# A pre-LN attention and SwiGLU block on one core: projection sums in row halves, and more of the score maxima moved ahead of attention

## The chip, the core and the metric

The kernel runs on one core of a Trainium2 chip. The metric is the device time of one execution in microseconds, the median over runs; lower is better.

## The reference

The input is one sequence of 2048 tokens of width 640. All arithmetic is float32.

```python
h  = x + mha(layernorm(x), wqkv, wo)        # 32 heads of width 20, softmax(q k^T / sqrt(20)) v
h2 = h + (silu(z @ w_gate) * (z @ w_up)) @ w_down      # z = layernorm(h), hidden width 1728
```

The softmax needs, for every query and head, the largest score over 2048 keys, to be subtracted before the exponential.

## The kernel before

Precision is kept by splitting each float32 operand into a high part in the matmul format `F32R` and a low part, so that each projection is a sum of three terms over five slices of 128 rows: 15 products of 128 rows.

There are three stages. In the **projections** (code in the block from line 252 to 556) the 2048 tokens are taken in four chunks of 512, `c` = 0 to 3. For each chunk a list `work` gives an order of 18 steps: ten blocks of 128 columns of queries or keys (`query_key`, line 416, matmul on line 424) and eight half value tiles (`value`, line 453, matmul on line 461). Each finished block is evicted by `keep`, split into high and low part, and stored to DRAM from the ScalarE queue; from there `stack` (line 136) loads it head by head into tiles of keys and queries, in which two heads share a matmul tile: one on rows 0 to 59 or 61, the other on rows 64 to 123 or 125. The next chunk's layer norm and its transposes (`flip`, line 389) are done between the steps.

In **attention** (from line 970) a unit `u` is one group of four heads with one chunk of 512 queries: 8 groups x 4 chunks = 32 units, of 16 key tiles each. Per key tile there are four score products of 128 keys by 512 queries (`scores`, line 890, matmul on line 895), four exponentials on ScalarE (line 901), and the weighting of the values (`weigh`, line 905), which runs two tiles later. The maximum is subtracted inside the score product: two extra rows of the query tile hold the negated maximum in high and low part, against rows of ones in the key tile, so all of a unit's maxima must be known before its first score.

The maxima need their own products, of 128 queries by 512 keys, reduced by VectorE. Counted per unit, key chunk `kc` of 512, query tile `t` and head pair `pair`, there are 1024 pairs (a pair is two heads, two products). `in_projections` (line 220) names those that are done during the projections by `max_pair` (line 166): two products into one tile of two PSUM banks, one reduction over 128x1024. There are 208 of them, on tiles of keys and queries staged early in the four `raw` buffers. `visit` (line 344) puts up to three of them after each step. The other 816 pairs, 1632 single products, are done by `max_one` (line 177) during attention, ahead of the unit that needs them.

The order in attention is written out by hand for each key tile by a string:

```python
ORDER = ("SmsSMMsWMm", "SsSmWmMs", "SssMWmS")
```

`s` and `S` are scores on the lower and the upper row half, `m` and `M` maxima on the lower and upper half, and `W` is the weighting together with the other work (weights for the next stage are prepared there too). Tile number modulo 3 chooses the string. When the maxima are used up the order is `sSsSW`. PSUM in this stage has four banks for scores, three for maxima, one for the weighting.

After attention come the output projection, the second layer norm and the feed-forward part, which the change does not touch. The order of the instructions on each engine is that of the program (`tc.manual_schedule()`).

Of the kernel before, what the change touches and what calls it, by code (L numbers as in the profile page):

```python
# [17 lines left out]
P = 128  # L18
# [3 lines left out]
DH = 20  # L22
# [17 lines left out]
ORDER = ("SmsSMMsWMm", "SsSmWmMs", "SssMWmS")  # L40
# [3 lines left out]
def tile_block(ctx: ExitStack, tc: tile.TileContext, x, wqkv, wo, wg, wu, wd, out):  # L44
# [21 lines left out]
    psum = ps_ctx.enter_context(tc.tile_pool(name="psum", bufs=1, space=bass.MemoryType.PSUM))  # L66

    def ps_wide():
        return psum.tile([P, 2, CH], F32, name="ps_wide", tag="ps_wide", bufs=3)

    def ps_one():
        return psum.tile([P, CH], F32, name="ps_one", tag="ps_one", bufs=2)
# [56 lines left out]
    def fill_ones(k):  # L129

        for b in range(2):
            nc.gpsimd.memset(k[b * ROW + ROW // 2 : (b + 1) * ROW].bitcast(F32), 1.0)
# [30 lines left out]

    mxs = {u: stk.tile([P, 2, 2, TPC, NC], F32, name=f"mx{u}") for u in range(NU)}

    def max_pair(mx, q, k, pair, t, kc, k0):

        ps = ps_wide()
        for b in range(2):
            rows = slice(b * ROW, b * ROW + NPART)  # L170
            nc.tensor.matmul(  # L171
                ps[:, b, :], q[rows, pair, t * P : (t + 1) * P], k[rows, pair, k0 : k0 + CH],
                start=True, stop=True,
            )
        nc.vector.tensor_reduce(mx[:, :, pair, t, kc], ps, axis=AX.X, op=ALU.max)  # L175
# [71 lines left out]

    def next_e():
        es.append(es.pop(0))
        return es[-1]  # L250

    with tc.tile_pool(name="pa", bufs=2) as pa:
# [18 lines left out]
        slot = [0]  # L271
        items, place, users = [], {}, {}

        def stored_at(which, g, c):

            block = ((g + 1) * GD - 1) // P
            if c == 0:
                return 2 * block + 4
            if c < NC - 1:
                return 18 * c + 3 + 3 * block + (0 if which else 1)  # L280
            return 18 * c + 3 + block + (0 if which else ND)
# [4 lines left out]
        def stage(use, which, g, c):  # L286
            place[which, g, use] = len(items)
            users[len(items)] = 0
            items.append([which, g, c, None, None])

        def load_items():
            for n, (which, g, c, loaded, _) in enumerate(items):
                if loaded is not None:
                    continue
                if slot[0] < stored_at(which, g, c) or (n >= 4 and users[n - 4]):
                    return
                t = raw_tile().rearrange("p a b -> p (a b)")[:, : 2 * CH].rearrange(
                    "p (h n) -> p h n", h=2
                )
                stack(t, which, g, slice(c * CH, (c + 1) * CH))  # L300
                items[n][3:] = t, slot[0]

        def staged_keys(g, c, kc):
            k, q = place[1, g, (c, kc)], place[0, g, c]

            def one(t, pair):
                max_pair(mxs[g * NC + c], items[q][3], items[k][3], pair, t, kc, 0)
                for n in (k, q):
                    users[n] -= 1
                load_items()  # L310

            def ready():
                return all(items[n][3] is not None and slot[0] >= items[n][4] + 2 for n in (k, q))

            pairs = [(t, pair) for t in moved(g * NC + c, kc) for pair in range(2)]
            for n in (k, q):
                users[n] += len(pairs)
            return [(ready, lambda a=a: one(*a)) for a in pairs]

        def unit_keys(u, kc, t, pair):  # L320
            max_pair(mxs[u], queries[u], keys[0], pair, t, kc, kc * CH)
            if u == 0 and (kc, t, pair) == (NC - 1, TPC - 1, 1):
                max_all(0)

        def in_unit(u, kc, at):
            return [
                (lambda: at <= slot[0], lambda t=t, pair=pair: unit_keys(u, kc, t, pair))
                for t in moved(u, kc) for pair in range(2)
            ]

        for g in range(1, NG):
            stage((0, 0), 1, g, 0)
            stage(0, 0, g, 0)
        for g in range(1, NG):
            stage((1, 0), 1, g, 0)
            stage(1, 0, g, 1)
            stage((1, 1), 1, g, 1)
        urgent = [a for kc in range(NC) for a in in_unit(0, kc, 18 * kc + 7)]
        early = [a for g in range(1, NG) for a in staged_keys(g, 0, 0)]
        early += in_unit(1, 0, 28) + in_unit(1, 1, 28)  # L340
        early += [a for g in range(1, NG) for kc in range(2) for a in staged_keys(g, 1, kc)]
        early += in_unit(2, 0, 46) + in_unit(2, 1, 46)

        def visit(n):
            load_items()
            for _ in range(n):
                for queue in (urgent, early):
                    if queue and queue[0][0]():
                        queue.pop(0)[1]()
                        break  # L350
# [13 lines left out]
        def split_w(m):  # L364
            cs = slice(m * P, (m + 1) * P)
            engine = nc.gpsimd if m % 2 == 1 else nc.vector
            split(raws.pop(m), w_hi[:, :, cs], w_lo[:, :, cs], engine)

        def norm(c):
# [4 lines left out]
            def apply(t):  # L374
# [9 lines left out]
                [lambda t=t: stats(pa, xs[c * TPC + t], mv[:, t, :]) for t in range(TPC)]  # L384
                + [lambda f=f, g=g: (f(), g()) for f, g in zip(steps[::2], steps[1::2])]
                + [lambda t=t: apply(t) for t in range(TPC)]
            )

        def flip(c, k):
            ps = ps_one()  # L390
# [4 lines left out]
            z_hi, z_lo = (z[:, k, :] for z in zs[c])  # L395
            split_sbuf(ps, z_hi, z_lo, next_e()[:, 0].bitcast(F32))
# [13 lines left out]
        def store(*last, queue=nc.scalar):  # L410

            while stores:
                queue.dma_start(*stores.pop(0))
            stores.extend(last)

        def query_key(c, *ms):

            z_hi, z_lo = zs[c]
            pss = [ps_one() for _ in ms]
            n = 0  # L420
            for a, w in ((z_hi, w_hi), (z_lo, w_hi), (z_hi, w_lo)):
                for ps, m in zip(pss, ms):
                    for k in range(ND):
# [4 lines left out]
                        if n == 1 and k == 3 and c:  # L428
                            visit(1)
                n += 1  # L430
            for ps, m in zip(pss, ms):
                keep(c, m, ps)

        def keep(c, m, ps):

            e = next_e()
            if slot[0] < 8:
                split(ps, e[:, 0], e[:, 1], nc.vector)
            else:
                split_sbuf(ps, e[:, 0], e[:, 1], e[:, 1].bitcast(F32))  # L440
            r0 = m // 2 * P
            pieces, r = [], r0
            while r < r0 + P:
# [3 lines left out]
                pieces.append(  # L447
# [1155 lines left out]
```

## Time and profile before

| | us |
|---|---|
| median of 3 runs | 2115.23 |
| lowest and highest run | 2113.74, 2119.4 |
| span of the profiled execution | 2118.2 |
| first score product of attention starts at | 343.1 |
| last copy of a weighted sum starts at | 1550.6 |

The page gives the profiled execution by its span alone; it lies 3.0 us above the median. In the rows below, PE is TensorE's matmuls, PEld its weight loads, DVE is VectorE, ACT ScalarE, POOL GpSimd, SP SyncE. A row of the timeline gives start, duration, engine, line, operation, tiles written and read, sizes, the count of merged instructions, and in brackets the idle time before it with what ended it. A row of the groups gives count, busy time and mean duration in ns, then idle time before. A row of the stretches gives, for each engine, busy time and number of instructions.

### The profile page before, as it was taken

How to read it: one execution, taken by the hardware profiler on the slowest of the kernel's cores; microseconds unless marked ns; L12 is line 12 of the kernel's file. 1: busy time of each engine (PE TensorE's matmuls, PEld its weight loads, DVE VectorE, ACT ScalarE, POOL GpSimd, SP SyncE). 2: the span in 40 equal slices, each digit the busy share in tenths (PEclk: the TensorE clock that was granted, in tenths of full speed). 3: DMA queues.
4: the chain of work that ended last, by engine and by line, in shares of the span. 5: the costliest groups of instructions: out<-in, count | busy, mean ns of one | idle time of the engine just before them, and what ended most of it. 6: DMA issues, size and time to landing. Idle time of an engine off the chain costs nothing.

```text
span 2118.2 us, 35577 instructions
## 1 busy us (share of the span) xinstructions
PE 2079.0 (98%) x12606; PEld 1205.0 (57%) x12606; DVE 1752.2 (83%) x2901; ACT 1295.4 (61%) x2571; POOL 705.0 (33%) x1009
## 2 busy tenths in 40 slices
PE   7998999999999999999999999999999999999998
PEld 5766675333333333333333333335578888888888
DVE  6998897999999999999999999996358766666677
ACT  3222215999999999999999999996743222212221
POOL 3221212244334433353420001001135534663555
PEclk9999999999999999999999999999999999999999
DMA  7555533333442534534332113132137755884542
GB/s 248 176 172 154 164 123 90 118 104 126 126 139 82 175 99 125 164 134 141 129 116 67 41 34 90 34 94 81 35 118 255 269 164 191 296 306 157 191 155 93
DMA packets 199673, 295.27 MB, mean 139 GB/s; under 512 B 46840, under 2 KB 81656, under 8 KB 198472
## 3 DMA queue, kind: packets, MB, share of 16 engines
q1 hardware_dynamic: 185912, 266.77, 38.9%
q10 hardware_dynamic: 13584, 26.23, 4.1%
q8 instruction: 101, 1.65, 0.3%
q14 instruction: 76, 0.62, 0.1%
HBM read 196.44 MB, written 95.68 MB: 138 GB/s over the span
## 4 chain that ended last, share of the span: by engine, by line
PE 87%; DVE 7%; DMA 4%; issue 1%; SPq 1%; ACT 1%; POOL 0%; ACTq 0%; POOLq 0%; DVEq 0%
PE acc L905 24%; PE ps_max L181 15%; PE ps_one L895 15%; PE ps_a L1068 14%; PE ps_b L1162 7%; PE ps_one L424 4%; DVE mx L175 4%; PE ps_max L633 2%; PE ps_wide L171 2%; PE ps_one L461 2%; DMA halves<-j_d 1%; PE ps_b L633 1%; DMA qk_d<-e 1%; DVE mx L187 1%; DMA units<-w_d 0%
## 5 line engine op out<-in xcount | busy, mean ns | idle before, releaser
L901 ACT ACTIVATE probs<-ps_one 128x512 f32<-128x512 f32 x2048 | 1045.2, 621 | 132.8 <-PE ps_one L895 128.1
L187 DVE TENSOR_REDUCE mx<-ps_max 128x1 f32<-128x512 f32 x1632 | 1020.5, 682 | 95.3 <-PE ps_max L181 52.8
L895 PE MATMUL ps_one<-q_stk,k_stk 62*128 62x512 f32 x2048 | 551.0, 421 | 0.7 <-ACT e L265 0.7
L905 PE MATMUL acc<-probs,v_stk 128*32 128x512 f32 x4096 | 546.1, 605 | 0.3
L181 PE MATMUL ps_max<-k_stk,q_stk 60*128 60x512 f32 x1632 | 541.3, 460 | 2.4 <-DVE mx L187 1.5
L181 PEld LDWEIGHTS ps_max<-k_stk,q_stk 60*128 60x128 f32 x1632 | 230.5, 184 | 429.3 <-DVE mx L187 413.1
L895 PEld LDWEIGHTS ps_one<-q_stk,k_stk 62*128 62x128 f32 x2048 | 300.0, 185 | 80.5 <-ACT probs L901 51.6
L175 DVE TENSOR_REDUCE mx<-ps_wide 128x2 f32<-128x1024 f32 x208 | 240.7, 1217 | 20.1 <-PE ps_wide L171 19.7
L1283 DVE TENSOR_TENSOR tmp<-ps_a,tmp 128x512 f32<-128x512 f32 x208 | 141.2, 689 | 120.3 <-PE ps_a L1068 94.5
L1162 PE MATMUL ps_b<-halves,yp 128*128 128x320 f32 x1032 | 179.3, 308 | 2.0 <-DMA halves<-j_d 1.3
L1162 PEld LDWEIGHTS ps_b<-halves,yp 128*128 128x128 f32 x1032 | 165.1, 188 | 18.6 <-POOL yp L81 1.5
L905 PEld LDWEIGHTS acc<-probs,v_stk 128*32 128x32 f32 x4096 | 80.7, 108 | 160.0 <-issue 152.0
L1068 PE MATMUL ps_a<-t,units 128*128 128x512 f32 x624 | 162.7, 396 | 0.0
L198 POOL CAST both<-neg 128x16 fp32r<-128x16 f32 x32 | 6.6, 208 | 466.8 <-DVE neg L194 222.8
L1068 PE MATMUL ps_a<-z,units 128*128 128x512 f32 x516 | 133.8, 394 | 0.0
L1068 PEld LDWEIGHTS ps_a<-t,units 128*128 128x128 f32 x624 | 112.6, 188 | 18.8 <-ACT tmp L1296 0.2
L81 POOL TENSOR_TENSOR yp<-y,yp 128x256 fp32r<-128x256 f32 x96 | 60.4, 629 | 188.2 <-ACT yp L80 188.2
L1167 DVE TENSOR_TENSOR h<-ps_b,h 128x320 f32<-128x320 f32 x248 | 110.0, 480 | 6.9 <-PE ps_b L1162 5.4
L1068 PEld LDWEIGHTS ps_a<-z,units 128*128 128x128 f32 x516 | 93.1, 187 | 15.9
L1068 PE MATMUL ps_a<-z,lasts 128*128 128x512 f32 x324 | 92.5, 393 | 0.0
L80 ACT ACTIVATE yp<-tmp 128x512 fp32r<-128x512 f32 x40 | 25.3, 632 | 103.2 <-POOL tmp L1155 103.2
L265 ACT ACTIVATE e<-ps_one 128x512 f32<-128x512 f32 x31 | 18.5, 598 | 105.4 <-PE ps_one L424 81.0
(164 smaller groups left out, 2066.1 us busy)
## 6 DMA issues: line engine op xcount, KB each, us to landing
units<-w_d SPq DMA_DIRECT2D x186, 256.0 KB
w_d<-stage SPq DMA_DIRECT2D x106, 256.0 KB
halves<-j_d SPq DMA_DIRECT2D x70, 320.0 KB
j_d<-stage SPq DMA_DIRECT2D x42, 320.0 KB
raw<-qk_d SPq DMA_DIRECT2D x70, 160.0 KB
k_stk<-qk_d SPq DMA_DIRECT2D x64, 160.0 KB
q_stk<-qk_d SPq DMA_DIRECT2D x64, 160.0 KB
rb<-r_d SPq DMA_DIRECT2D x32, 256.0 KB
```

The source lines that it names most:

```text
L175: nc.vector.tensor_reduce(mx[:, :, pair, t, kc], ps, axis=AX.X, op=ALU.max)
L181: nc.tensor.matmul(ps, queries[u][rows, pair, t * P : (t + 1) * P], keys[u // NC][rows, pair, kc * CH : (kc + 1) * CH], start=True, stop=True,
L187: nc.vector.tensor_reduce(mxs[u][:, b, pair, t, kc : kc + 1], ps, axis=AX.X, op=ALU.max)
L424: nc.tensor.matmul(ps, w[:, k, m * P : (m + 1) * P], a[:, k, :], start=(n == 0 and k == 0), stop=(n == 2 and k == ND - 1),)
L633: nc.tensor.matmul(ps[:, :HALF], a[:, k, :], w[:, k, hs], start=(n == 0), stop=(n == 3 * ND - 1),)
L895: nc.tensor.matmul(ps, keys[u // NC][rows, p, kt * P : (kt + 1) * P], queries[u][rows, p, :], start=True, stop=True,)
L901: nc.scalar.activation(probs[p][:, b, :], ps, AF.Exp, scale=scale)
L905: nc.tensor.matmul(acc[32 * j : 32 * j + 32, :], values[u // NC][:, kt, j * VW : j * VW + 32], probs[j // 2][:, j % 2, :], start=(kt == 0) ...
L1068: nc.tensor.matmul(ps.rearrange("p (t n) -> p t n", t=TPC), w[k][:, i], z[k][:, :, j], start=(first and m == 0), stop=(last and m == len(n ...
L1162: nc.tensor.matmul(ps, a, b, start=(n == 0), stop=(n == len(pairs) - 1))
L1167: nc.vector.tensor_tensor(out=h, in0=ps, in1=h, op=ALU.add)
L1283: add = lambda out, ps, x: nc.vector.tensor_tensor(out=out, in0=ps, in1=x, op=ALU.add)
```

## The change

**Projections, sums.** Each product of 128 rows becomes two products of 64 rows, rows 0 to 63 and 64 to 127 of the same operands. A sum is a job: first its 15 lower halves, then its 15 upper halves, into the same PSUM bank. The first upper half waits for an empty instruction on ScalarE, which waits for the last lower half. A class `Halves` writes out the order: it keeps a planned time for each row half and engine, issues the upper halves of one job between the lower halves of the next, and puts products for maxima in wherever its plan has banks free. The first two blocks stay whole.

**Projections, maxima.** For two keys a and b, max(q·a, q·b) = q·a + max(0, q·(b - a)). GpSimd subtracts one half of the staged keys from the other: within a chunk (72 pairs: ScalarE takes the positive part of 256 columns, VectorE adds the other 256 and takes the maximum in one pass), or one chunk from another (224 pairs' worth: one product with the differences, 512 columns through ScalarE, a second product with the plain keys, added and maximised by VectorE). 296 pairs' worth are done here instead of 208, on more places for staged keys: four quarters of the still unused key tile among them.

**Projections, queues.** PSUM is cut into five single banks and three for sums. The stores of blocks and values go out from the SP queue instead of ScalarE's.

**Attention.** 728 pairs are left, 1456 single products. Each key tile has three maxima, in six orders whose row halves alternate from one product to the next. The rest of attention is as before.

```diff
-ORDER = ("SmsSMMsWMm", "SsSmWmMs", "SssMWmS")
+ORDER = ("sMsSmSmW", "SmMsMsSW", "mSmMsSsW")
+ORDER += tuple(a.swapcase().replace("w", "W") for a in ORDER)
...
+    def max_differences(mx, q, k, pair, t, kc, place):
+
+        pss = max_products(q, k, pair, t, 0)
+        more = place.rearrange("p (i n) -> p i n", i=2)
+        for b, ps in enumerate(pss):
+            nc.scalar.activation(more[:, b], ps[:, CH // 2 :], AF.Relu)
+        for b, ps in enumerate(pss):
+            nc.vector.tensor_tensor_reduce(
+                out=more[:, b], in0=ps[:, : CH // 2], in1=more[:, b], scale=1.0, scalar=LEAST,
+                op0=ALU.add, op1=ALU.max, accum_out=mx[:, b, pair, t, kc : kc + 1],
+            )
+
+    def max_twice(mx, q, first, more, pair, t, kc, b, place):
...
+        def second():
+            product(pss[1], first)
+            nc.vector.tensor_tensor_reduce(
+                out=place, in0=pss[1], in1=place, scale=1.0, scalar=LEAST,
+                op0=ALU.add, op1=ALU.max, accum_out=mx[:, b, pair, t, kc : kc + 1],
+            )
+
+        product(pss[0], more)
+        nc.scalar.activation(place, pss[0], AF.Relu)
+        return second
...
-        if u == 0 or (u == 2 and kc < 2) or (c < 2 and kc == 0):
+        if u == 0 or (c == 1 or u == 2) and kc < 2:
             return True
-        return c == 1 and kc == 1 and t < (2 if g < NG // 2 else 3)
+        return c == 0 and kc <= (2 if g % 2 else 0)
...
+            def issue(self, half):
+                job = next(j for j in self.jobs if j["at"][half] < j["n"])
+                i = job["at"][half]
...
+                rows = slice(half * ROW, (half + 1) * ROW)
+                lhs, rhs, out = job["step"](i, rows)
+                product = nc.tensor.matmul(
+                    job["ps"][:, :out], lhs, rhs,
+                    start=(half == 0 and i == 0), stop=(half == 1 and i == job["n"] - 1),
                 )
...
+                self.stream(half, out / 2217)
+                if half == 0 and job["at"][0] == job["n"]:
+                    job["after"] = nc.scalar.nop().ins
+                    behind(job["after"], product.ins)
...
+                if half == 1 and job["at"][1] == 1:
+                    behind(product.ins, job["after"])
...
+            def run(self, c, n, step, done):
+                job = dict(c=c, n=n, step=step, done=done, at=[0, 0], ps=None)
+                self.jobs.append(job)
...
+                while job["at"][0] < n:
+                    half = int((self.second[1] or self.may_follow()) and self.t[1] <= self.t[0])
+                    if self.second[half]:
+                        self.finish_second(half)
+                    else:
+                        self.issue(half)
+                    self.pair()
...
-        def store(*last, queue=nc.scalar):
-
+        def store(*last, queue=nc.sync):
...
-        def query_key(c, *ms):
+        def query_key(c, m):
 
             z_hi, z_lo = zs[c]
...
+            def step(i, rows):
+                a, w = terms[i // ND]
+                return w[rows, i % ND, cs], a[rows, i % ND, :], CH
+
+            pe.run(c, 3 * ND, step, lambda ps: keep(c, m, ps))
...
-            order = ORDER[now[0] % 3] if singles[0] or singles[1] else "sSsSW"
+            order = ORDER[now[0] % len(ORDER)] if singles[0] or singles[1] else "sSsSW"
```

More of the change, by code (lines that the diff above doesn't have):

```diff
@@ L334, in tile_block @@
[L334 to L350, printed above, removed]
+        own_places = [None, quarters[0]]
@@ L352, in tile_block, with behind @@
+        def behind(ins, other):
+            tc.add_manual_dep(
+                ins, other.name,
+                mybir.DependencyInfo(mybir.DependencyClass.Sync, mybir.DependencyReason.DATA),
+                reason="the second half after the first",
+            )
+        pe = Halves()
+        landed = {(i, g, c): 0 for i in range(2) for g in range(NG) for c in range(NC)}
         raws = {}
@@ L476, in tile_block @@
+            pe.run(c, 3 * ND, step, done)
         load_x(0)
         fill_ones(k_stk[0])
+        for u in range(NU):
+            if any(moved(u, kc) for kc in (1, 2)):
+                nc.gpsimd.memset(mxs[u], LEAST)
         for i in range(4):
```

457 lines of the change are left out of this document (349 added, 108 removed).

## The prediction

> **What bounds the kernel now.** I read the busy time by stretch first, then the timeline of each stage. The change touches the projections (start to 343 us) and attention (343 to 1551 us); what follows is untouched.
>
> ```profile
> core 0: us, PE busy (x) PEld busy (x) DVE busy (x) ACT busy (x) POOL busy (x), PEclk, DMA share, GB/s
> 0.00:50.00 50.00, 38.32 (x152) 28.10 (x152) 32.21 (x71) 18.11 (x27) 19.07 (x16) 0.97 0.80 253
> 50.00:343.10 293.10, 279.30 (x1433) 197.59 (x1431) 259.55 (x281) 71.95 (x129) 60.00 (x48) 0.99 0.51 155
> 100.00:150.00 50.00, 47.24 (x229) 31.20 (x230) 48.92 (x67) 10.36 (x18) 9.03 (x7) 1.00 0.61 182
> 300.00:320.00 20.00, 19.87 (x123) 15.41 (x123) 19.90 (x19) 3.00 (x8) 0.42 (x2) 1.00 0.15 59
> 379.00:451.00 72.00, 71.98 (x490) 28.05 (x489) 66.24 (x110) 65.29 (x131) 26.86 (x50) 1.00 0.41 124
> L187 DVE TENSOR_REDUCE mx<-ps_max 128x1 f32<-128x512 f32 x1632 | 1020.5, 682 | 95.3 <-PE ps_max L181 52.8 <-PE ps_one L895 27.9 <-ACT e L80 10.5
> ```
>
> In the projections' rows from 100 and from 300 us DVE is 98 and 99% busy while ACT does 21 and 15%: the maxima set the pace there. In attention PE never stops, DVE is at 92% and ACT at 91%. Three engines at that level hold each other up, so I go to the single key tile. W (line 905, the weighting) closes each tile.
>
> ```profile
> 700.42 1.06 PE L905 MATMUL acc<-probs,v_stk 128*32 128x512 f32 x8
> 701.42 0.19 PEld L181 LDWEIGHTS ps_max<-k_stk,q_stk 60*128 60x128 f32 x2 [0.84 <-DVE mx L187]
> 701.42 0.50 PE L181 MATMUL ps_max<-k_stk,q_stk 60*128 60x512 f32 x2
> 701.95 3.78 DVE L187 TENSOR_REDUCE mx<-ps_max 128x1 f32<-128x512 f32 x6 [0.22 <-PE ps_max L181]
> 702.32 1.06 PE L905 MATMUL acc<-probs,v_stk 128*32 128x512 f32 x8
> 703.32 0.51 PE L181 MATMUL ps_max<-k_stk,q_stk 60*128 60x512 f32 x2
> 704.08 4.52 ACT L901 ACTIVATE probs<-ps_one 128x512 f32<-128x512 f32 x9 [0.33 <-PE ps_one L895]
> 704.45 1.06 PE L905 MATMUL acc<-probs,v_stk 128*32 128x512 f32 x8
> 705.44 0.49 PE L181 MATMUL ps_max<-k_stk,q_stk 60*128 60x512 f32 x1
> 707.14 1.07 PE L905 MATMUL acc<-probs,v_stk 128*32 128x512 f32 x8
> 154.59 0.97 PE L171 MATMUL ps_wide<-k_stk,q_stk 60*128 60x512 f32 x6
> 384.73 0.63 ACT L915 ACTIVATE o<-acc 128x512 f32<-128x512 f32 x1
> 858.50 0.68 ACT L915 ACTIVATE o<-acc 128x512 f32<-128x512 f32 x1
> ```
>
> Three tiles run from W at 700.42 to W at 707.14: 6.72 us, 2.24 a tile. W itself holds PE 1.00 us (702.32 to 703.32). Between the W's stand the products over 60 to 62 rows: 6 in 0.90 us (701.42 to 702.32), 7 in 1.13, 9 in 1.70 (705.44 to 707.14). A lower-half and an upper-half product run side by side: the two loads at 701.42 take 0.19 us together and the two products 0.50. Three pairs take 0.97 (154.59), so one more pair costs (0.97 - 0.50)/2 = 0.235 us, which I call a slot. By the orders on line 40 the gap of 6 is M m S s S m, three slots, 0.70; that of 7 is m M S s S s M, four slots, 0.94; both leave about 0.2 for switching to W. The gap of 9 (m S S m s S M M s) has five slots and should take 1.37; it takes 0.33 more. That is the stall: five maxima in one tile for three PSUM banks, at (3.78 - 0.68)/5 = 0.62 us of DVE each (0.68 being one reduction, line 187). Between units there is more: 13 units of 16 tiles from 384.73 to 858.50 are 36.44 us each, of which 16 x 2.24 = 35.84 are tiles and 0.60 the unit's own work.
>
> **Attention after.** Each of the six new orders has four scores and three maxima, halves strictly alternating. Seven products are four slots, so the gap should be the 1.13 us of today's gap of 7, and the tile 2.13. DVE needs 3 x 0.62 = 1.86 us of it; ACT needs four exponentials at (4.52 - 0.62)/8 = 0.49, 1.95 us. Both fit, and the maxima come one by one, so the 0.33 us stall goes. What is late next is PE itself, with ACT 0.18 us behind. A unit becomes 16 x 2.13 + 0.60 = 34.7 us, 1.76 less; over the 30 units before the output projection mixes in, 53 us. The ends: nothing, if the three engines go on stalling each other, and ACT's 1.95 us, if W's switch hides (another 16 x 0.18 x 30 = 86 us). I take the 2.13 because that gap of 7 is measured with the same products. Maxima finish no later: 1456 at 3 a tile last 485 tiles, as 1632 at 10 in 3 lasted 490, and the tightest unit keeps 5 tiles in hand in both. Attention's DMAs and the weight preparation hang on tiles, not on time; they move closer together at a DMA share of 0.41.
>
> **Projections after: PE.** The changed kernel's PE queue holds two whole blocks, 38 block sums and 32 value sums as 30 half products each, 296 pairs of max products (72 by differences inside a chunk, 224 by differences between two chunks) and 60 transposes.
>
> ```profile
> 13.22 1.59 PEld L402 LDWEIGHTS ps_wide<-ident,xt 128*128 128x128 f32 x14 [0.56 <-issue]
> 17.18 2.56 PE L424 MATMUL ps_one<-z_hi,w_hi 128*128 128x512 f32 x10 [0.79 <-ACT z_hi L80]
> 28.08 1.30 PE L424 MATMUL ps_one<-z_hi,w_hi 128*128 128x512 f32 x5
> 29.22 1.30 PE L424 MATMUL ps_one<-z_lo,w_hi 128*128 128x512 f32 x5
> 149.91 0.66 PE L392 MATMUL ps_one<-ident,xt 128*128 128x128 f32 x4
> 150.32 1.40 PE L424 MATMUL ps_one<-z_hi,w_hi 128*128 128x512 f32 x5
> 294.82 0.89 PE L461 MATMUL ps_one<-w_lo,z_hi 128*128 128x320 f32 x5
> 295.55 0.90 PE L461 MATMUL ps_one<-w_hi,z_lo 128*128 128x320 f32 x5
> 343.10 0.49 PE L895 MATMUL ps_one<-q_stk,k_stk 62*128 62x512 f32 x1 [0.69 <-ACT e L265]
> ```
>
> Five block products follow in 1.14 us (28.08 to 29.22), 0.228 each; five value products in 0.73, 0.146 each; a flip takes 0.41 (149.91 to 150.32). Before: 17.2 us to the first block, 40 x 15 x 0.228 = 137, 32 x 15 x 0.146 = 70, 208 x 0.235 = 49, 15 x 0.41 = 6: 279 of the 343.1 us; 64 are waits. After, if halves pair like the maxima: 88 more pairs, 21 us, so 300 with no waits at all. Two half products of the same length cost one whole one, so the halves by themselves gain nothing; they let a single half max product fill in.
>
> **Projections after: DVE, ACT, POOL, SP.**
>
> ```profile
> L175 DVE TENSOR_REDUCE mx<-ps_wide 128x2 f32<-128x1024 f32 x208 | 240.7, 1217 | 20.1 <-PE ps_wide L171 19.7
> L1283 DVE TENSOR_TENSOR tmp<-ps_a,tmp 128x512 f32<-128x512 f32 x208 | 141.2, 689 | 120.3 <-PE ps_a L1068 94.5 <-POOL yp L81 14.7 <-ACT tmp L1296 4.5
> L1185 DVE TENSOR_TENSOR own<-ps_b,own 128x320 f32<-128x320 f32 x128 | 56.7, 481 | 2.5 <-PE ps_b L1162 2.4
> L80 ACT ACTIVATE yp<-y 128x256 fp32r<-128x256 f32 x96 | 30.6, 362 | 78.8 <-DVE y L1287 66.8 <-DMA units<-w_d 8.4 <-PE ps_b L1162 3.5
> L81 POOL TENSOR_TENSOR e<-e 128x512 fp32r<-128x512 f32 x22 | 28.4, 1291 | 122.2 <-ACT e L80 86.2 <-DMA raw<-qk_d 31.1 <-PE ps_wide L171 4.8
> 0.82 0.06 DVE L77 MEMSET eps_t<- 128x1 f32 x1 [0.82 <-PEq L1586]
> 9.02 0.17 DVE L90 TENSOR_SCALAR v_a<-mv 128x4 f32<-128x4 f32 x1
> 9.23 0.17 DVE L90 TENSOR_SCALAR r_a<-v_a 128x4 int32<-128x4 int32 x1
> 145.77 7.53 SPq L143 DMA_DIRECT2D raw<-qk_d  x8
> 146.03 1.35 ACTq L413 DMA_DIRECT2D qk_d<-e  x3
> ```
>
> DVE's 208 reductions go (240.7 us). In come 224 add-and-max passes over 512 columns and 144 over 256, each followed by a write of its 128x1 result. No pass of that kind is in this trace. From below: the reduction's 0.62 us, 0.34 for half the columns (0.62 less 256 x 1.08 ns, the slope between the tensor-tensor rows of 512 and 320 columns), result hidden: 139 + 49 = 188 us. From above: 0.69 and 0.41 plus a small operation's step of 0.21 (9.02 to 9.23): 202 + 89 = 291 us. I take 0.06 (the smallest write) on top of the mean of the two prices, 0.72 and 0.44, 225 us, since 128x1 is nearest to the memset: less DVE than today, for 296 pairs instead of 208. [...]
>
> ACT gets 224 relus of 512 at 0.49 and 144 of 256 at about 0.30 (0.362 less overlap), 153 us, in a stage where it was idle for four fifths; it loses the issue of 107 stores (0.45 each, row at 146.03), 48 us. POOL gets 37 subtractions, 48 us at 1.29, and 14 small memsets while it is idle at the start. SP gets the 112 stores and 248 instead of 168 loads; at 7.53/8 = 0.94 us, waits included, that is at most 340 us, and at 0.45 net 160 us. Behind a store that waits for POOL's low part stand the loads of the next keys; the products wait for those. I cost it at nothing while the net figure holds; the cover is the time between a load and its first use.
>
> The added waits: a sum's second half waits for an empty instruction on ACT, which itself waits for the end of the first half. Behind it on PE stands everything; on ACT, relus and evictions. It is hidden while the next sum's first half has products to issue. The swap of the PSUM pool at the start costs under 1 us, the wait for the last eviction of the first flips.
>
> From 50 us on DVE has 259.6 - 240.7 = 19 us of other work and ACT 72, so the sums there are 244 for DVE and 225 for ACT. PE needs 300 over the whole stage. No engine is full any more, but the queues are in order. I let half of today's 64 us of waits stay: 300 + 32 = 332, 11 us less than 343, which leaves DVE at 244 of 282 us. The ends are 300 (43 less) and 364 (21 more).
>
> **The sum.** The profiled execution has a span of 2118.2 us, 3.0 above the 2115.23 median of the runs. 2118.2 - 53 - 11 = 2054; on the median's scale 2051.
>
> **Rivals.**
> - DVE stays the bound of the projections: at the upper price 291 + 19 = 310 us after the first 50, at the 97% of its busiest stretches 320. The rows at 98 and 99% speak for it, the memset's 0.06 against it. Stage 370 us, 38 more than I forecast: 2089. Chance 0.15.
> - Weight loads bound the halves. Where loads set the pace, one follows the other in (1.59 - 0.19)/13 = 0.108 us (13.22). If the two halves' loads queued, a value sum would take 30 x 0.108 = 3.24 us for 2.19, 34 us over 32 sums: 2085. The two loads in 0.19 us at 701.42 speak against it. [...] Chance 0.05.
> - Attention falls to ACT's pace, 2.05 a tile or less: another 40 to 86 us, near 2000. Today's tiles of 1.90 speak for it; they live on the slower tile before them. Chance 0.07.
> - Slower: the handover between halves. 70 sums each wait for ACT, which now has about 2.2 us of relus per sum in front. If PE finds no other half product, each sum loses that: it eats the 64 us gained from 0.9 us per sum on, and at 2 us adds 140: 2190. For it speaks that PE's queue is in order, against it that the next sum's fifteen first halves fill 3.4 us. Chance 0.12.
> - The change does not do what it says: attention keeps 2.24 a tile and the projections their 343: 2115. Chance 0.03.
>
> **The numbers.** My forecast has the remaining 0.58: 2051, by itself 2025 to 2075. The range 2010 to 2098 takes in the DVE and load rivals and leaves out 0.22 or slightly less. Measurement can tell about 0.3% (6 us) from no change. Faster: 0.58 + 0.15 + 0.05 + 0.07 = 0.85; same 0.03; slower 0.12.
>
> **What would show it.** In the profile after: W to W 2.13 us in all tiles with maxima, units of 34.7 us, PE's waits for attention's reductions gone; first score near 332 us; the new passes near 0.72 and 0.44 us apart and DVE below 90% in the projections; load pairs of the halves together in 0.19 us. The forecast is wrong if W to W stays above 2.2, if the first score comes after 364 us, or if PE's waits at the second halves reach 0.9 us per sum.

## The result, and the profile after

After: 2080.53 us, median of 4 runs (2077.16 to 2086.12). Before, on the same chip: 2115.86 (2113.74 to 2119.4). The ratio is 0.9833, 95% interval 0.981 to 0.9856: about 35 us faster, where 64 were forecast. The profiled execution spans 2084.3 us against 2118.2, 33.9 less. The changed kernel's is the slowest of its four (2086.12), 5.6 us above the median, so figures of its trace lie some us high. Three kernels of experiments 5 and 6 have the same projections as the changed one; their first scores come at 365.7, 367.7 and 368.5, so a first score is good to about 4 us.

Busy time of the changed kernel by stretch (columns as named in the first row):

```profile
core 0: us, PE busy (x) PEld busy (x) DVE busy (x) ACT busy (x) POOL busy (x), PEclk, DMA share, GB/s
50.00:369.70 319.70, 298.59 (x2593) 264.12 (x2593) 228.06 (x811) 237.78 (x499) 126.85 (x105) 0.94 0.59 181
159.00:176.10 17.10, 16.10 (x137) 13.94 (x135) 8.74 (x26) 13.09 (x24) 6.46 (x5) 1.00 0.49 148
176.10:186.30 10.20, 5.82 (x40) 5.83 (x41) 2.71 (x8) 4.24 (x8) 3.78 (x3) 0.50 0.40 109
369.70:1522.00 1152.30, 1148.04 (x7915) 466.02 (x7916) 961.11 (x1610) 1084.80 (x2141) 326.34 (x533) 1.00 0.33 104
```

The two stages went opposite ways. Attention's first score comes at 369.70 instead of 343.1: the projections are 26.6 us longer, where 11 less were forecast. From there to the last copy of a weighted sum (1520.7, before 1550.6) attention takes 1151.0 us instead of 1207.5, 56.5 less, about as forecast. What follows is 4.0 shorter. In the projections PE's granted clock is 0.94 in place of 0.99, and for 10.2 us it is 0.50.

Attention, the timeline of PE over three key tiles (W is line 1235, scores 1225, maxima 223):

```profile
700.10 1.07 PE L1235 MATMUL acc<-probs,v_stk 128*32 128x512 f32 x8
702.22 1.06 PE L1235 MATMUL acc<-probs,v_stk 128*32 128x512 f32 x8
703.21 0.49 PE L1225 MATMUL ps_one<-q_stk,k_stk 62*128 62x512 f32 x1
703.22 0.73 PE L223 MATMUL ps_max<-k_stk,q_stk 60*128 60x512 f32 x2
704.34 1.06 PE L1235 MATMUL acc<-probs,v_stk 128*32 128x512 f32 x8
706.45 1.06 PE L1235 MATMUL acc<-probs,v_stk 128*32 128x512 f32 x8
771.97 0.50 PE L1225 MATMUL ps_one<-q_stk,k_stk 62*128 62x512 f32 x1
775.71 0.47 PE L223 MATMUL ps_max<-k_stk,q_stk 60*128 60x512 f32 x1 [2.70 <-DMA q_stk<-qk_d]
```

From 700.10 to 706.45 three tiles take 6.35 us, 2.12 each, and PE has no wait in them; 2.12 is the median in each of the six orders. The first 28 units are 34.1 to 35.5 us but for one of 39.18, that of the last row: there a maximum waited 2.70 us for queries that had not landed, and 3.4 us of half clock followed.

The new passes on DVE, 512 columns (line 210) and 256 (line 193):

```profile
211.93 0.69 DVE L210 CUSTOM_DVE_ANT_0 q_stk<-ps_single,q_stk 128x512 f32<-128x512 f32 x1
212.54 0.08 DVE L210 DVE_READ_ACCUMULATOR2_ANT mx<- 128x1 f32 x1
212.54 0.69 DVE L210 CUSTOM_DVE_ANT_0 v_stk<-ps_single,v_stk 128x512 f32<-128x512 f32 x1
62.16 0.42 DVE L193 CUSTOM_DVE_ANT_0 v_stk<-ps_single,v_stk 128x256 f32<-128x256 f32 x1
62.51 0.08 DVE L193 DVE_READ_ACCUMULATOR2_ANT mx<- 128x1 f32 x1
62.51 0.42 DVE L193 CUSTOM_DVE_ANT_0 v_stk<-ps_single,v_stk 128x256 f32<-128x256 f32 x1
```

One follows the other in 0.61 and 0.35 us. The read of the accumulator (0.08) starts with the next pass and adds nothing to that: the plain reductions of 512 columns before followed each other in 0.62.

What PE's weight loads waited for in the projections (total us, times, longest), first before, then after:

```profile
PEld ps_wide L171 <- DVE mx L175: 29.4, 60, 2.2
PEld ps_wide L171 <- issue: 13.3, 51, 0.5
PEld ps_one L424 <- issue: 11.0, 44, 0.4
```

```profile
PEld ps_single L180 <- DVE mx L193: 7.5, 6, 3.2
PEld ps_one L498 <- ACT v_stk L311: 5.8, 2, 5.6
PEld ps_single L204 <- ACT e L311: 4.9, 2, 4.3
PEld ps_single L204 <- DVE mx L210: 4.3, 16, 0.9
PEld ps_one L498 <- issue: 2.7, 13, 0.4
```

Before, the waits were many and short: 60 for reductions, and some hundred "issue" waits at changes between products of 128 and of 60 rows. Both are mostly gone. In their place stand a few long ones, of which several end on ACT's evictions. Two weight loads of different row halves run side by side, as the prediction expected, 0.19 us for both:

```profile
287.17 0.19 PEld L498 LDWEIGHTS ps_one<-z_lo,w_hi 64*128 64x128 f32 x1
287.17 0.19 PEld L498 LDWEIGHTS ps_one<-z_hi,w_lo 64*128 64x128 f32 x1
```

The longest wait, in the rows of ACT, SP and POOL around it:

```profile
165.28 3.16 SPq L151 DMA_DIRECT2D k_stk<-qk_d  x4
166.69 0.60 ACT L311 ACTIVATE v_stk<-ps_one 128x512 f32<-128x512 f32 x1 [0.28 <-issue]
168.03 1.29 POOL L89 TENSOR_TENSOR v_stk<-v_stk 128x512 fp32r<-128x512 f32 x1 [1.23 <-ACT v_stk L88]
168.49 4.25 SPq L151 DMA_DIRECT2D raw<-qk_d  x8
173.07 1.70 SPq L691 DMA_DIRECT2D qk_d<-v_stk  x2
173.23 0.63 ACT L88 ACTIVATE z_hi<-e 128x512 fp32r<-128x512 f32 x1
179.83 0.60 ACT L311 ACTIVATE v_stk<-ps_one 128x512 f32<-128x512 f32 x1 [5.97 <-DMA qk_d<-v_stk]
```

A block is evicted at 166.69 into the third of three rotating buffers (it lies in the tile `v_stk`), its low part is ready at 169.3, its store issued only at 173.07, and the next eviction that draws this buffer waits for the landing until 179.83. PE stops from 174.79 to 180.48, and its clock is halved from 176.1 to 186.3 (the row above).

The stage also has a new end. Behind the last product of the sums, at 359.40, the order still holds 21 max products, and the first score comes 10.3 us later; before the change none was left there, and it came 1.1 us later. The clock is halved again from 363.84, although no step from one product's start to the next in the 6.9 us before is longer than 0.95 us:

```profile
363.10 5.61 PE L204 MATMUL ps_single<-raw 60*128 60x512 f32 x14 [0.20 <-ACT q_stk L216]
363.84:369.70 5.86, 4.87 (x13) 2.81 (x13) 5.18 (x16) 4.18 (x7) 0.00 (x0) 0.50 0.25 71
```

This half clock lasts until 377.5, 7.8 us into attention.

For the accounts below I split PE's time from the first block product (at 17.2 us before, 17.9 after) to the first score into steps over 0.6 us from one product's start to the next ("pauses"), the time at half clock outside them, and the rest, at full clock. A straight-line fit of the steps to the kinds of product gives the pace per product in us; it moves by 0.01 to 0.03 with the length of the stretches that are fitted.

| | first score | pauses (count) | half clock | rest | pace: block, value, max |
|---|---|---|---|---|---|
| before (whole sums) | 343.1 | 21.9 (17) | 6.8 | 297.2 | 0.243, 0.149, 0.20 |
| after (halves) | 369.7 | 31.1 (17) | 31.2 | 289.5 | 0.133, 0.076, 0.105 |

Before, 416 max products at 0.20 are 83 us of PE; after, 592 at 0.105 are 62. Pairing works. What the stage loses is pauses and half clock: 9 and 24 us more.

### The profile page after: what moved, and what is told of

Its sections match the earlier page's. It is cut to its first block, busy times and chain, and to the rows that moved or that the text cites. A ratio compares the mean times of both kernels' runs of the same rounds, so it can differ in the third digit from the quotient of the medians.

```text
span 2084.3 us, 39077 instructions
## 1 busy us (share of the span) xinstructions
PE 2037.9 (98%) x13656; PEld 1245.0 (60%) x13656; DVE 1617.8 (78%) x3251; ACT 1471.6 (71%) x2941; POOL 774.7 (37%) x1082
## 4 chain that ended last, share of the span: by engine, by line
PE 89%; DMA 7%; DVE 1%; issue 1%; POOL 1%; SPq 1%; ACT 1%; POOLq 0%; ACTq 0%; DVEq 0%
PE acc L1235 24%; PE ps_one L1225 16%; PE ps_a L1398 15%; PE ps_max L223 11%; PE ps_b L1492 8%; PE ps_one L498 7%; PE ps_single L204 3%; PE ps_max L963 2%; DMA k_stk<-qk_d 1%; PE ps_b L963 1%; DMA raw<-qk_d 1%; DMA halves<-j_d 1%; DMA q_stk<-qk_d 1%; DMA qk_d<-e 1%; PE ps_single L180 1%
## 5 line engine op out<-in xcount | busy, mean ns | idle before, releaser
L1231 ACT ACTIVATE probs<-ps_one 128x512 f32<-128x512 f32 x2048 | 1057.6, 611 | 66.5 <-PE ps_one L1225 26.3
L229 DVE TENSOR_REDUCE mx<-ps_max 128x1 f32<-128x512 f32 x1456 | 915.7, 684 | 124.9 <-PE ps_max L223 76.4
L1225 PE MATMUL ps_one<-q_stk,k_stk 62*128 62x512 f32 x2048 | 586.5, 432 | 1.0 <-DVE mx L210 1.0
L223 PE MATMUL ps_max<-k_stk,q_stk 60*128 60x512 f32 x1456 | 486.1, 440 | 3.4 <-DMA q_stk<-qk_d 3.4
L1225 PEld LDWEIGHTS ps_one<-q_stk,k_stk 62*128 62x128 f32 x2048 | 289.8, 186 | 291.3 <-ACT probs L1231 269.6
L223 PEld LDWEIGHTS ps_max<-k_stk,q_stk 60*128 60x128 f32 x1456 | 241.4, 185 | 169.2 <-DVE mx L229 131.6
L210 DVE CUSTOM_DVE_ANT_0 q_stk<-ps_single,q_stk 128x512 f32<-128x512 f32 x158 | 105.7, 689 | 50.9 <-ACT q_stk L216 40.1
L498 PE MATMUL ps_one<-z_hi,w_lo 64*128 64x512 f32 x380 | 104.5, 401 | 0.0
L216 ACT ACTIVATE q_stk<-ps_single 128x512 f32<-128x512 f32 x158 | 91.6, 596 | 17.8 <-PE ps_single L204 9.4
L1270 POOL TENSOR_TENSOR o<-o,rb 128x512 f32<-128x512 f32 x31 | 39.9, 1286 | 164.7 <-DMA q_stk<-qk_d 84.3
```

What stands on the lines that cost most here:

```text
L210: nc.vector.tensor_tensor_reduce(out=place, in0=pss[1], in1=place, scale=1.0, scalar=LEAST, op0=ALU.add, op1=ALU.max, accum_out=mx[:, b, p ...
L216: nc.scalar.activation(place, pss[0], AF.Relu)
L223: nc.tensor.matmul(ps, queries[u][rows, pair, t * P : (t + 1) * P], keys[u // NC][rows, pair, kc * CH : (kc + 1) * CH], start=True, stop=True,
L229: nc.vector.tensor_reduce(mxs[u][:, b, pair, t, kc : kc + 1], ps, axis=AX.X, op=ALU.max)
L498: product = nc.tensor.matmul(job["ps"][:, :out], lhs, rhs, start=(half == 0 and i == 0), stop=(half == 1 and i == job["n"] - 1),)
L1225: nc.tensor.matmul(ps, keys[u // NC][rows, p, kt * P : (kt + 1) * P], queries[u][rows, p, :], start=True, stop=True,)
```

## The experiments

**1. The stores' queue.** Theory Q blamed the move of the stores to SP.

```diff
-        def store(*last, queue=nc.sync):
+        def store(*last, queue=nc.scalar):     # second kernel: nc.gpsimd
```

> The changed kernel with one word altered: the projections' stores are issued from ACT's queue again, as before the change, instead of SP's. Theory Q (queue): on SP a store stands behind loads that themselves wait, an eviction buffer comes free late, ACT's next eviction waits for it (5.97 us at 175 us into the changed kernel), PE runs dry and its clock is halved afterwards; so the first score comes at 335 to 350 us instead of 369.7, and the whole takes 2045 to 2065 us. Theory M (the plan's assumed times are too short wherever the stores are issued) and theory W (the stage is simply that much work): first score within 5 us of 369.7, time within 6 us of 2080.

> The changed kernel with the projections' stores on GpSimd's queue. Theory Q: no loads are ahead of the stores here, only the low parts and the subtractions of keys, so the first score comes at 340 to 360 us and the whole takes 2050 to 2070 us. Theories M and W: first score within 5 us of 369.7, time within 6 us of 2080. If an issue on this queue is dear for GpSimd itself (it also makes the low parts that PE needs), the stage is longer than 370 us.

Third, the kernel before with its stores on SP:

> The kernel before with the projections' stores issued from SP's queue, nothing else altered. Theory Q: its first score moves from 343 to 353 to 373 us, with new waits of ACT's evictions for stores. Theory M: within 5 us of 343, since its own plan leaves the buffers time enough. A result in between (5 to 10 us) says that the queue alone costs something and the rest comes from the fuller plan.

ACT's queue: 2105.08 us (0.9942, 0.9918 to 0.9965), first score 386.9. GpSimd's: 2116.87 (0.9995, 0.9979 to 1.0012), first score 396.3. Before with SP stores: first score 341.6, 2118.96 in one run. Q falls: away from SP the changed kernel is 25 and 36 us slower, and SP costs the old one nothing that one run shows. Theories M and W, by which the queue makes no difference, missed for the changed kernel as well: its first score comes 17 and 27 us later. With ACT's queue, waits of ACT (totals), and the same buffer again:

```profile
ACT q_stk L216 <- POOL z_lo L89: 8.9, 2, 6.4
ACT v_stk L311 <- DMA qk_d<-v_stk: 5.7, 1, 5.7
172.77 0.79 ACTq L691 DMA_DIRECT2D qk_d<-v_stk  x2
179.01 0.60 ACT L311 ACTIVATE v_stk<-ps_one 128x512 f32<-128x512 f32 x1 [5.67 <-DMA qk_d<-v_stk]
```

ACT's relus (line 216) now wait for low parts that POOL makes; no relu reads those, a store in front of it in ACT's queue does. And the wait for this buffer's store to land is there whichever queue issues it: 5.97 us from SP, 5.67 from ACT's, 9.47 from GpSimd's (there the eviction starts at 189.37). So the queue alone does not make it late.

**2. Issue sooner.** Two ways to shorten the time from low part to store: on SP as soon as the plan takes the data to be ready, and on GpSimd right behind the low part.

```diff
             def issue(self, half):
+                if stores and self.now() >= due[0]:
+                    store()
...
             store(*pieces)
+            due[0] = max(free, pe.free["pool"]) + 0.3
...
```

```diff
-            store(*pieces)
-            kept[id(e)] = 1
+            store()
+            for dst, src, what in pieces:
+                nc.gpsimd.dma_start(dst, src)
+                landed[what[0]] += what[1]
```

> The changed kernel with each of the projections' stores issued on SP as soon as the plan takes its data to be ready, instead of with the next sum's end or when its buffer comes round again. In the changed kernel and in the one with ACT's stores alike, the pause at 175 us follows a store issued 1 us before its buffer is wanted, so ACT waits out the whole landing (5.97 and 5.67 us). Theory D (late issue): the pauses at 72, 148, 175 and 305 us (1.8, 4.2, 5.7 and 2.8 us) go, with the half clock behind them (about 12 us lost), so the first score comes at 345 to 356 us and the whole takes 2055 to 2068. Theory S (the store meets a busy SP queue or busy DMAs whenever it is issued): first score within 5 us of 369.7, time within 6 us of 2080.

> The changed kernel with each block's stores issued on GpSimd right behind the low part that GpSimd has just made, so that they wait neither for SP's loads nor for the next sum's end; values' stores stay on SP. Theory D (what hurts is the time from the low part to the issue): the pauses at 72, 148, 175 and 305 us shrink by 2 to 4 us each, first score 352 to 362, the whole 2062 to 2074. If GpSimd's issue takes its time from the low parts and the differences of keys (80 issues at about 0.6 us, 48 us), pauses that end on GpSimd's operations appear instead and the first score is over 370.

The first: 2090.02 (0.9868, 0.9846 to 0.989), first score 375.6; the second 2091.04 (0.9883, 0.9862 to 0.9905), 376.5. Theory D falls in both, and theory S, which had the time unchanged within 6 us, missed as well. On SP the store still leaves at 172.62 behind twelve loads and the pauses at 149, 175 are as before; the one at 201 us grows from 1.6 to 4.9, ending on differences of keys whose eight loads take SP 6.87 us to issue instead of 5.05. On GpSimd five of the pauses over 1.3 us end on its own operations (one in the changed kernel), as the second branch of the expectation had it. There the store of the buffer at 175 us leaves right behind its low part, and still the eviction waits 5.0 us for the landing, 9.3 us after the first issue:

```profile
171.66 1.19 POOL L747 DMA_DIRECT2D qk_d<-v_stk  x2 [0.29 <-POOL v_stk L89]
180.97 0.60 ACT L311 ACTIVATE v_stk<-ps_one 128x512 f32<-128x512 f32 x1 [5.00 <-DMA qk_d<-v_stk]
```

An early issue does not make this buffer free in time.

**3. The ring.** Leave the time of issue alone; take the transposed blocks out of the buffers.

```diff
-                self.single.append([self.use("scalar", 0.5, self.now() + 0.4) + 0.2])
-                self.use("scalar", 0.48)
-                self.use("pool", 1.3, self.free["scalar"] + 0.1)
+                seen = self.use("scalar", 0.5, self.now() + 0.4)
+                self.single.append([self.use("vector", 0.68, seen + 0.1) + 0.2])
...
-            split_sbuf(ps, z_hi, z_lo, next_e()[:, 0].bitcast(F32))
+            split(ps, z_hi, z_lo, nc.vector)
```

The first lines are the plan's booking of a transposed block: it changes with the edit, and with it the order of products that the plan writes out.

> The changed kernel, with the transposed blocks of x split straight from PSUM (high part by ACT, low part by DVE) instead of through a copy in one of the three eviction buffers. Theory R (the ring): in chunks 1 to 3 two transposes and one block go through three buffers, so a block's buffer comes round again one block later, before its store has landed; taken out of the ring, the pauses at 148 and 175 us (4.2 and 5.7 us) and the half clock behind them (17 us long, 8 lost) go, those at 72 and 305 us, where blocks follow blocks, stay. First score 350 to 358, the whole 2060 to 2070. DVE gets 15 x 0.69 = 10 us more, POOL 19 less. Theory S (stores wait for SP and busy DMAs, whatever the ring): first score within 5 us of 369.7, time within 6 us of 2080.

2063.38 us (0.9751, 0.9736 to 0.9765), first score 349.39. Theory R held, with a first score just below its range. Waits of ACT for stores between 50 and 350 us, the changed kernel's first, then this kernel's, with PE's longest wait and the stage:

```profile
ACT e L311 <- DMA qk_d<-e: 8.1, 2, 5.7
ACT v_stk L311 <- DMA qk_d<-v_stk: 6.0, 1, 6.0
ACT z_hi L311 <- DMA qk_d<-z_hi: 3.2, 1, 3.2
```

```profile
ACT e L311 <- DMA qk_d<-e: 1.9, 1, 1.9
ACT v_stk L311 <- DMA qk_d<-v_stk: 0.9, 1, 0.9
ACT ev L761 <- DMA v_d<-ev: 4.6, 2, 3.3
PEld ps_one L1224 <- DVE mx L210: 3.2, 1, 3.2
50.00:349.39 299.39, 286.28 (x2592) 256.51 (x2593) 237.91 (x826) 229.06 (x485) 107.98 (x90) 0.98 0.62 192
```

The waits for stores out of the ring, 17.3 us, became 2.8; new are 4.6 us for the stores of values, which have buffers of their own (`ev`). In the changed kernel the four waits of the first list ended PE's pauses at 72, 148, 175 and 305 us, 14.5 us together. Of these the second and third are gone, the first is 1.3 us, and the one at 305, expected to stay, lost its wait for a store (3.0 us are left there, behind a relu). All pauses fall from 31.1 to 19.9 us (11), half clock from 31.2 to 10.2, the clock rises to 0.98; PE's products still take 301 us at full clock. Of the 20.3 us that the first score gained, 11.2 are pauses and 10.5 the half clock's loss (half of 31.2 less 10.2); the rest of the stage gives back 0.8, and it starts 0.6 later. By the medians of the runs the gain is 17.2.

Not all of it is the ring's. 13.6 us are gained up to the last product of the sums, where the pauses for stores were. The other 6.7 lie behind it: the new order leaves 3 max products there instead of 21, and then PE waits 3.2 us for DVE's last maxima (last row but one). The edit also takes 15 splits off ACT and POOL. A fourth buffer with the old order would separate these; it was not run.

**4. Halves or whole sums.** The halves are taken back, and with them the empty instruction; all else stays.

```diff
-                rows = slice(half * ROW, (half + 1) * ROW)
-                lhs, rhs, out = job["step"](i, rows)
+                lhs, rhs, out = job["step"](i, slice(0, P))
...
```

> The changed kernel with its block and value sums as whole products of 128 rows again, with no handover between halves; maxima, plan and attention unchanged. Theory P (pairing): outside pauses a max product takes 0.105 us on PE after the change and 0.20 before it, because a lone half product only finds a partner among half products; without halves 592 of them cost 56 us more and the sums some 12 us less, so the first score comes at 400 to 420 us and the whole takes 2110 to 2135. Theory H (the handover eats the halves' gain): the first score comes before 365 us.

2383.59 us in one run, first score 662.0. P has the sign, and its price was far too low. Stretches of this kernel:

```profile
50.00:190.00 140.00, 138.32 (x584) 83.50 (x582) 81.13 (x341) 82.90 (x204) 48.65 (x39) 0.97 0.54 167
191.50:345.00 153.50, 153.50 (x305) 74.79 (x304) 52.29 (x158) 51.62 (x90) 20.30 (x17) 0.50 0.24 74
358.70:638.00 279.30, 279.30 (x565) 137.24 (x565) 89.03 (x279) 95.98 (x173) 43.23 (x39) 0.50 0.18 55
```

At full clock the max products stand mostly in twos between products of 128 rows (71 of the 93 groups up to 190 us), where the kernel before had them in groups of up to six; they cost 0.37 us each by the same fit, 0.33 if the others are priced as before. 592 of them are 195 to 219 us instead of 62. From 191 us on the clock stays at half for 433 us in all, though PE counts as busy for the whole of it. The plan was made for halves, so this run says what the change needs, not what whole sums could reach at their best.

**5. Attention's order.** Same number of maxima, spread otherwise.

```diff
-ORDER = ("sMsSmSmW", "SmMsMsSW", "mSmMsSsW")
-ORDER += tuple(a.swapcase().replace("w", "W") for a in ORDER)
+ORDER = ("SmsSMMsWMm", "SsSmWMs", "SssMWmS")     # and its mirror: 5, 2, 2
+ORDER = ("ssmmSSMW", "SSMMssmW")                 # another kernel: halves in blocks
```

> The changed kernel with nine maxima in three key tiles as 5, 2 and 2 instead of 3, 3 and 3. Theory of banks (five maxima in one tile wait for three PSUM banks): the tile with five takes 2.70 us and the others 1.90, units 35.3 us instead of 34.4, so the whole is about 25 us longer: 2105. Rival (only the count matters): units 34.4 to 34.7 and the time 2080.

> The changed kernel with attention's order of a key tile altered so that lower and upper halves do not alternate (s s m m S S M W and its mirror): same four scores and three maxima in each tile. Theory of slots (two products of different halves share a slot of 0.235 us, two of the same half do not): fewer pairs, so W to W is about 2.6 us instead of 2.13, units about 42 us, and the whole about 2310. Rival (only the number of maxima per tile matters, not their halves): W to W stays 2.13 and the time 2080.

Uneven: 2109.76 us in one run, 29 more than the changed kernel; tiles with five maxima have a median of 2.71 us, those with two 1.92, units 35.5. The theory of banks held. Blocks: 2110.78 in one run, tiles 2.16 and 2.22, units a median of 35.5. Neither theory has that. A tile of this kernel, whose program order is two scores and two maxima of one half, then two scores and a maximum of the other:

```profile
704.17 1.06 PE L1234 MATMUL acc<-probs,v_stk 128*32 128x512 f32 x8
705.16 0.74 PE L1224 MATMUL ps_one<-q_stk,k_stk 62*128 62x512 f32 x4
705.74 0.63 PE L222 MATMUL ps_max<-k_stk,q_stk 60*128 60x512 f32 x3
706.30 1.06 PE L1234 MATMUL acc<-probs,v_stk 128*32 128x512 f32 x8
```

All four scores start ahead of the first maximum, as in 350 of 456 tiles: the second pair of scores ran past two maxima that stand before it in the program. A tile then takes the four slots of its fuller half, not those of its pairs in program order, and strict alternation is worth 0.04 to 0.10 us a tile, not 0.47.

**6. Queries earlier, and both edits together.**

```diff
-            if kt == 6 and u + 3 < NU:
+            if kt == 2 and u + 3 < NU:
```

> The changed kernel, with the queries of the unit three ahead loaded at key tile 2 instead of 6 of a unit. If the single unit of 39.18 us (W to W at 771 to 776 us) is long because maxima that run three units ahead meet queries that have not landed, that unit falls to 34.4 us, no other changes, and the whole is 5 us shorter: 2075. If the long unit has another cause, it stays at 39 us and the time at 2080.

> The two edits that helped, together: transposed blocks split straight from PSUM, and attention's queries loaded at key tile 2 instead of 6. The first took 17 us off alone. The unit that the late queries stretch was 39.18 us in the changed kernel, 34.88 with the early load, but only 35.89 with the direct splits alone; so between 1 and 5 us more: 2058 to 2063 us, first score within 3 us of 349.4, all units from 34.0 to 35.6 us.

Alone: the unit of 39.18 takes 34.88, and from the first score to the end it is 1708.9 us instead of 1714.6; the one run takes 2079.21. With the direct splits: 2062.66 (0.975, 0.9731 to 0.9768), first score 349.86; within what can be measured that is the 2063.38 of the splits alone. Both versions beat both kernels.

**7. The plan's landing time.** On top of that, `at + 6.5` becomes `at + 8.5` in the two places where the plan takes a load to have landed.

> As the run before, with the plan of the projections taking 8.5 instead of 6.5 us from a load's issue to its landing, so that maxima on loaded keys and queries are put later on PE. Theory M (the plan's assumed landing is too short and PE meets keys that are not there yet): the pauses at 46 and 182 us that end on GpSimd's differences of keys (1.7 and 2.3 us) and the half clock behind them go, first score 340 to 346, the whole 5 to 9 us less than the run before. Rival (starved plan: fewer maxima are ready when a half is free, so halves run alone): first score 3 to 15 us later than in the run before.

In this kernel one of the 224 passes between chunks still uses its place in the values' tile when group 0's values are loaded there, so part of the values differs from the reference; kinds and numbers of operations are the same. 2071.72 us (0.9786, 0.977 to 0.9801), first score 362.6, 12.7 later: pauses 30.0 us and half clock 22.8 again, with 13 max products behind the sums; by the medians 9.1 us are lost. M falls for this constant, the rival held: waiting longer in the plan starves it.

## Why the prediction was right in direction and short in size

The time of 2080.53 misses the 2025 to 2075 that the forecast gave for itself; it lies in the wider range because that took in the DVE and the weight load rival, and neither came about. The first score of 369.7 is the 370 of the DVE rival, with DVE 71% busy: both are luck. By the prediction's own sign (a first score after 364) its account of the projections is wrong.

**Attention, right.** W to W 2.12 for 2.13, the ordinary unit 34.4 for 34.7. From the first copy of a weighted sum to the thirtieth, 29 units take 1009.0 us instead of 1060.3: 51.3 for the 53 of 30 units, with 4.7 lost on the one late load. The uneven order shows that the count alone is not it: nine maxima as 5, 2, 2 give back about half of the gain per unit (medians 36.46 before, 35.5 uneven, 34.4 after). "Attention's DMAs hang on tiles, not on time" was the small miss: the queries are issued at the same tile, but faster tiles left the load less time. The old gap of 7 is, by the order strings, m M s S s s M and not as the prediction lists it; its fuller half has four either way.

**DVE, at the lower bound.** 0.61 and 0.35 us per pass, not 0.72 and 0.44: 224 and 144 of them are 187 us, not 225. DVE is busy 228 of 320 us (71%) and the rival of a DVE bound has no support. What the prediction put on top of a pass for its result, 0.06, was its estimate; in the trace the accumulator's read takes 0.08 and lies under the next pass.

**Weight loads, no bound.** In stretches of value halves alone the products follow each other in 0.077 us (median), less than the 0.108 that one load after the other would take, and two loads take 0.19 us side by side. The rival priced a load of 64 rows like one of 128, and by itself it is as long: 188 to 200 ns on average (line 498) against 187 to 188 (line 1398). What the trace does not show is that the two halves' loads queue.

**The handover, hidden.** The 70 first upper halves can be told in the trace by the semaphore that their weight loads wait for. PE's step at such a load is 0.12 us on average and at most 0.43. The rival put 0.9 us per sum there.

**"Half of today's 64 us of waits stay" is the step that failed.** It carried the whole gain of the projections. Three things are wrong in it. First, I took the waits for one pool, to shrink with DVE's load. By the accounts above the 64 were 39 of slower pace (unpaired products, changes of rows), 22 of pauses and 3 of half clock. Secondly, after the change each moved its own way: pace costs 22 us over the paired minimum of 283, so 16 less; pauses 31, so 9 more; half clock's loss 16, so 12 more. The 69 together stand where 32 were forecast. Thirdly, nothing in my sum had the clock: in the trace of before it cost 3 us, while the pause of 5.7 us at 175 us leaves PE at half speed for 5.8 us after its end, another 2.9 lost. Nor did it have the end of the stage: 10.3 us from the last product of the sums to the first score instead of 1.1.

**The stores and their buffers.** I asked whether loads behind a store would be late, and costed it at nothing. The store itself was late for its buffer, whichever queue issued it and whether it left at once or not (experiments 1 and 2). What it is late for is the ring of three buffers that blocks and transposed blocks share: at the new pace it comes round before a store has landed. With the transposed blocks taken out, 20 of the 37.7 us between forecast (332) and result (369.7) are back, 13.6 of them where the pauses for stores were. Of the remaining 17, 16 are this version's 23 of pace, 20 of pauses and 5 of half clock's loss less the 32 I had left; the rest is a start 1.3 us later than in my sum. Which part of the pace is lost to products of unequal length (512 columns against 320) and which to the ends of sums no run separates.

## What to carry to other kernels

Split a stage's lost time into pace, pauses and clock before saying which share an edit will win: they answer to different causes. When a stage gets denser, look for the resource whose turn-round was hidden by the old pace (here three eviction buffers and a store's landing), and count what else passes through it; using it less worked where earlier issue and three queues did not, though part of that gain came with a new order of products. In order-bound code spread the work that needs few banks evenly (5, 2, 2 maxima instead of 3, 3, 3 cost 29 us here).

## What the runs showed of the hardware

Around the projections of thirteen traces (all but that of the whole sums of experiment 4) the half clock comes in spells of 3.4, 6.8, 10.2, 13.7 or 17.1 us. There all 26 pauses of 3.5 us or more had a spell running by 3.4 us after their end; of those from 2.0 to 3.5 us, 26 of 44 had. One of 2.25 us by itself was followed by a spell (experiment 3), one of 3.47 (stores on GpSimd) was not. So from 2.0 to 3.5 us the length of a pause does not by itself tell whether the clock falls. Pauses are not all of it. In experiment 4 the clock is at half for 433 us though PE counts as busy throughout, and at the end of the projections, in seven traces, a spell of 10.2 to 17.1 us begins with no step over 0.95 us in the 6.9 us before. In both places products of 60 rows run singly or in small groups; whether that holds the clock down is open.

The prediction has "PE's queue is in order"; in these traces matmuls do not always start in the program's order. In experiment 5 all four scores start ahead of the first maximum in 350 of 456 tiles, two of them past maxima on other rows that precede them. In the changed kernel's six alternating orders 391 of 466 tiles start in the program's order, and in 74 a score is ahead of a maximum that precedes it. Whether PE or the last step of the build changed the order no run tells.
